# Decay attention followed by a feed-forward layer: q and k loads issued earlier, second product two units behind the first and by halves of the tokens

## The chip, the cores and the metric

The kernel runs on one core of a Trainium2 chip. The metric is device microseconds of one execution. The profile is of one profiled execution of the same program. Names of engines in the profile: PE (TensorE matmul), PEld (its weight loads), DVE (VectorE), ACT (ScalarE), POOL (GpSimd), SP (SyncE, which issues all the DMAs here).

## The reference

Eight batches of eight heads, 576 tokens, head size 64. The attention output, 4608 tokens of 512, goes through a feed-forward layer with 2048 hidden units.

```python
# q, k, v: (8, 8, 576, 64); f: (8, 8, 576)
scores = np.matmul(q, k.transpose(0, 1, 3, 2)) / np.sqrt(64)
cum = np.cumsum(np.log(np.clip(f, 1e-4, 1.0)), axis=-1)
scores = np.where(causal, -1e9, scores + cum[..., :, None] - cum[..., None, :])
attn = np.exp(scores - scores.max(-1, keepdims=True))
x = (attn / (attn.sum(-1, keepdims=True) + 1e-9)) @ v   # -> (4608, 512)
h = x @ w_in                                            # (4608, 2048)
g = np.where(h >= 1, h, np.where(h <= -1, 0, (h + 1) ** 2 / 4))
out = g @ w_out                                         # (4608, 512)
```

## The kernel before, in words

**Attention by jobs.** A job is one pair of heads of one batch (in batch 0 the rows are cut in two, so that there are 36 jobs: eight in batch 0, four in each later batch). The first jobs compute in float32. From job 12 on, q and k are quantized into a high and a low half in float16. For such a job the steps are:

- `load` (L326) brings q and k into one of two float32 buffers, `qk32[ji % 2]`, with six DMAs: for q two of L347 and one of L351, for k the same.
- `measure` (L390) sums the squares of q and of k on ACT (L397, one instruction each, which writes `m2q`); PE adds them over the partitions (L128), and DVE makes a scale of it (L129 to L137). Its result is `sc`.
- `prepare` (L408) quantizes: ACT writes the high halves (L414, two instructions on q and k with the scale `sc`), DVE the low halves (L416), and one DMA transpose brings both into `qkT` (L421). After L416 the q and k buffer is free for the load after the next.
- `load_decay` (L355) brings one head's row of the sums of the log decay to all partitions as `ck` (three buffers); `split_values` (L427) loads v (two DMAs of L440, one of L442) and splits it (L447 on ACT, L448 on DVE).
- For each of five row blocks `r`, `scores` (L459) multiplies q and k into PSUM (tile `s`, two buffers) and has POOL write decay and causal mask (L488, L492) into `sdr` (four buffers) or `sd4` (two, for the last block). `weights` (L557) adds both and takes the row minimum on DVE (L571, which writes `nm`), exponentiates on ACT (L575), makes the reciprocal of the sum on DVE (L583, L586, `rc`), and writes the weights' high half on ACT (L589) and low half on DVE (L595) into `pr`. A DMA transpose (L601, for the last block two of L604) turns them into `pT`, of which there is one buffer.
- `values` (L608) multiplies with v (L615) and writes the result into `x` (L624, L625).

**Feed-forward by units.** A unit is 256 tokens (a chunk) by 256 hidden units (a block), eight units to a chunk, 144 in all. `moe_front` (L642) is the first product, 24 matmuls of 256 columns (48 shorter ones where a chunk lies in two batches) into PSUM tile `ph` (L657). Then comes the chain ACT L666 (relu), ACT L667 (square), DVE L668 (which is the last to read `ph`), ACT L670 (high half of `g`), DVE L671 (low half of `g`). `moe_back` (L678) is the second product: twelve matmuls of 512 columns (L685) from `g` into two PSUM tiles `po0` and `po1`, one for each half of the chunk's tokens, summed over the chunk's eight units. After the last, ACT evicts both (L702) and the chunk is stored (L705). `ph` has two buffers, shared with the sums over partitions (L118, L128); `g` has two; `po0` and `po1` one each.

**What sets the order.** `moe_unit` (L710) issues the first product of a unit and then the second product of the unit before. The loop over jobs (L759) issues, in job `p`: the load of job `p + 2`, `prepare` of job `p + 1`, the row blocks of job `p`, after the last of them `measure` of job `p + 2`, and between the row blocks `values` of job `p - 1` and a share of the units whose tokens are ready: four a job in most batches, six in some. What is left of the units follows after the last job. This is the order in which the code is written. A list scheduler in the framework then sets the order on each engine: it takes the instructions in the order of the code, but lets one whose inputs and buffers are free (by its own estimate) go ahead of one that has to wait. On the chip each engine then follows its list, and SP issues the DMAs in the order of its own.

Of the kernel before, what the change touches and what calls it, by code (L numbers as in the profile page):

```python
# [8 lines left out]
F32 = mybir.dt.float32  # L9
F16 = mybir.dt.float16  # L10
I32 = mybir.dt.int32
AF = mybir.ActivationFunctionType
ALU = mybir.AluOpType
AX = mybir.AxisListType

P = 128
# [29 lines left out]
def kernel(  # L46
# [19 lines left out]
    nc = tc.nc  # L66
# [80 lines left out]
    def decay_sums():  # L147
        fl = early
        nb = B * H
        nc.sync.dma_start(fl[0:nb, 0:S], f.rearrange("b h s -> (b h) s"))  # L150
        nc.vector.tensor_scalar(
            out=fl[0:nb, 0:S], in0=fl[0:nb, 0:S], scalar1=1e-4, scalar2=1.0, op0=ALU.max, op1=ALU.min
        )
        nc.scalar.activation(fl[0:nb, S:2 * S], fl[0:nb, 0:S], AF.Ln)
        nc.gpsimd.memset(fl[0:nb, 3 * S:4 * S], 0.0)
        cum = fl[0:nb, 2 * S:3 * S]
        nc.vector.tensor_tensor_scan(
            out=cum, data0=fl[0:nb, S:2 * S], data1=fl[0:nb, 3 * S:4 * S], initial=0.0, op0=ALU.add, op1=ALU.add
        )
        nc.sync.dma_start(cum_d, cum)  # L160
        pt = ps.tile([P, 1024], F32, name="s")
        twice = fl[0:nb, 0:P]
        nc.vector.tensor_copy(
            twice.rearrange("p (a b) -> p a b", a=2), cum[:, FULL:S].unsqueeze(1).broadcast_to([nb, 2, 64])
        )
        for t in range(NT5):
            nc.tensor.transpose(
                pt[:, nb * t:nb * t + nb], cum[:, P * t:P * t + P] if t < LAST else twice, ident[0:nb, 0:nb]
            )
        nc.vector.tensor_copy(cq.rearrange("p t n -> p (t n)"), pt[:, 0:NT5 * nb])  # L170

# [197 lines left out]
    squares = bits.bitcast(F16)[:, 0:2 * NT5 * D]  # L369
    cq8 = const.tile([P, NT5, 2 * H], F32, name="cq8")  # L370

    def early_prepare(w):

        if w.p == 0:
            nc.vector.tensor_scalar(out=cq8, in0=cq[:, :, 0:2 * H], scalar1=8.0, scalar2=None, op0=ALU.mult)
        t_ = early_qk[(w.p + NQK) % 2]
        w.nsig, w.nalpha = -8.0, -0.125
        bh = w.b * H + 2 * w.hp
        w.cqs = cq8[:, :, bh:bh + 2]
        w.terms = ((t_[:, 0], t_[:, 1]),)  # L380
# [9 lines left out]
    def measure(w):  # L390
# [14 lines left out]
        w.cqs = tiny.tile([P, NT5, 2], F32, name="cqs")  # L405
        nc.vector.tensor_scalar(out=w.cqs, in0=cq[:, :, bh:bh + 2], scalar1=w.nsig, scalar2=-1.0, op0=ALU.mult, op1=ALU.mult)

# [234 lines left out]
    def moe_front(ch, fb):  # L642
# [25 lines left out]
        nc.vector.scalar_tensor_tensor(out=u, in0=h, scalar=z.t[:, i:i + 1], in1=u, op0=ALU.max, op1=ALU.min)  # L668
        g = two.tile([P, 2, 2 * TC], F16, name="g")
        nc.scalar.activation(g[:, 0], u, AF.Copy, scale=z.r[:, i:i + 1])  # L670
# [7 lines left out]
    def moe_back(ch, fb, g, z):  # L678
        first, last, part = z.first == fb, z.last == fb, z.first > 0
        if first:  # L680
            po[ch] = [ps1.tile([P, DM], F32, name=f"po{i}") for i in range(2)]
        for fi in range(2):
            for i in range(2):
                for gl, wl in ((0, 0), (0, 1), (1, 0)):
# [25 lines left out]
    def moe_unit(ch, fb):  # L710
        pending.append(moe_front(ch, fb))
        if len(pending) > 1:
            moe_back(*pending.pop(0))
# [43 lines left out]
    value_scale(0)  # L757
    split_values(pairs[0])
    for p in range(njobs + 1):  # L759
        w = pairs[p] if p < njobs else None  # L760
        nxt = pairs[p + 1] if p + 1 < njobs else None
        steps = []
        if w:
            if w.b not in xs:
                xs[w.b] = xpool.tile([P, NPAIR, 2, S], F16, name="x")
            if p + 2 < njobs:
                pairs.append(load(p + 2))
            if nxt:
# [4 lines left out]
            def step(r):  # L773
                if r + 1 < w.r1:
                    scores(w, r + 1)
                if r == w.r1 - 2 and nxt:
                    load_decay(nxt, 1)
                    split_values(nxt)
                weights(w, r)
                if w.r1 == NT5 and w.b + 1 < B:  # L780
                    n = w.r1 - w.r0
# [69 lines left out]
```

## Time and profile before

| | |
|---|---|
| median of 3 runs | 1209.1 us (1208.8 to 1213.09) |
| profiled execution | 1206.77 us, span 1205.0 us |
| PE busy | 1047.8 us (87%) |
| ACT busy | 795.6 us (66%) |
| DVE busy | 789.7 us (66%) |
| POOL busy | 418.1 us (35%) |
| granted clock of TensorE, mean | 0.94 |
| DMA, hardware queue | 150.63 MB, 57.7% of 16 engines' span |

How to read it: PE's share is a mean over unlike stretches. Up to about 210 us the weights are converted and the first jobs run, and PE is busy for 132.48 us of 210. From there to about 1050 us jobs and units run side by side. The rest is units alone. A row of the waits gives engine, tile and line of the one that waited, the one that it waited for, the total in us, how often, and the longest. In a timeline row stand start and duration in us, then engine, line, operation, tiles, shape, count, and in brackets the idle time ahead of it with the one that ended it.

### The profile page before, as it was taken

The page shows a single profiled execution, that of the slowest core. Times are in us where ns is not written, and L with a number is a line of the kernel's source. Part 1 is how long each engine was busy: PE and PEld are TensorE (multiplying, and loading weights), DVE is VectorE, ACT ScalarE, POOL GpSimd, SP SyncE. Part 2 cuts the span into 40 slices and gives each one's busy share as a digit, 9 for nine tenths or more (in the row PEclk, how much of TensorE's full clock was granted, in tenths as well). Part 3 has the DMA queues.
Part 4 walks back from the last instruction along what each step waited for, and adds up shares of the span by engine and source line. Part 5 has one row for each costly group of instructions (what it writes and reads, how often), then busy time and mean ns, then how long its engine had stood idle before and what let it go on. Part 6 is the DMA issues. An engine that isn't in the chain of part 4 may idle for free. (4 is left out here: it accounts for less than half of the span.)

```text
span 1205.0 us, 24383 instructions
## 1 busy us (share of the span) xinstructions
PE 1047.8 (87%) x8809; PEld 664.8 (55%) x8809; DVE 789.7 (66%) x2103; ACT 795.6 (66%) x1638; POOL 418.1 (35%) x679
## 2 busy tenths in 40 slices
PE   4666765988978889898898998999898999999998
PEld 2433443554645556555655655555565566667665
DVE  5769989787767667765566666676677686532222
ACT  4566876577867677776566667777677686644443
POOL 4467764234533233333213323342343343100000
PEclk9666888998989999998999999999899999999999
DMA  7868788479857566854633745675668575300000
GB/s 226 271 173 243 166 208 180 111 160 181 170 118 169 113 134 127 155 112 111 126 69 76 144 87 130 117 155 116 129 127 149 106 139 105 73 19 1 18 18 18
DMA packets 408281, 152.18 MB, mean 126 GB/s; under 512 B 383968, under 2 KB 384992, under 8 KB 408160
## 3 DMA queue, kind: packets, MB, share of 16 engines
q1 hardware_dynamic: 408160, 150.63, 57.7%
q8 instruction: 69, 1.13, 0.4%
q14 instruction: 52, 0.43, 0.1%
HBM read 75.64 MB, written 9.58 MB: 71 GB/s over the span
## 5 line engine op out<-in xcount | busy, mean ns | idle before, releaser
L685 PE MATMUL po<-place,g 128*128 128x512 f16 x1728 | 429.5, 393 | 55.0 <-ACT g L670 39.4
L657 PE MATMUL ph<-x,place 128*128 128x256 f16 (+3 forms) x4608 | 420.7, 248 | 24.0 <-DVE u L668 24.0
L657 PEld LDWEIGHTS <-place 128*128 128x128 f16 x4608 | 354.2, 98 | 94.2 <-issue 38.5
L685 PEld LDWEIGHTS <-g 128*128 128x128 f16 x1728 | 165.0, 100 | 245.2 <-ACT g L670 56.3
L488 POOL TENSOR_SCALAR sdr<-ck,nsig,cqs 128x128 f32<-128x128 f32 (+1 forms) x192 | 147.3, 771 | 151.2 <-DVE pr L595 148.7
L575 ACT ACTIVATE sdr<-sdr,nm 128x384 f32<-128x384 f32 (+1 forms) x248 | 137.9, 557 | 75.9 <-DVE nm L571 75.3
L668 DVE SCALAR_TENSOR_TENSOR u<-ph,z,u 128x512 f32<-128x512 f32 x136 | 101.6, 747 | 129.4 <-ACT u L667 129.2
L488 POOL TENSOR_SCALAR sd<-ck,nsig,cqs 64x576 f32<-64x576 f32 x48 | 44.2, 921 | 341.6 <-ACT sdr L575 191.6
L666 ACT ACTIVATE u<-ph,z 128x512 f32<-128x512 f32 x136 | 104.4, 768 | 88.0 <-PE ph L657 88.0
L482 PE MATMUL s<-qkT 64*64 64x512 f16 (+11 forms) x1056 | 129.6, 351 | 35.3 <-DVE nm L571 24.9
L595 DVE SCALAR_TENSOR_TENSOR pr<-sdr,rc,pr 128x384 f16<-128x384 f32 (+2 forms) x232 | 129.9, 596 | 41.1 <-ACT pr L589 40.1
L670 ACT ACTIVATE g<-u,z 128x512 f16<-128x512 f32 x136 | 97.8, 719 | 79.0 <-DVE u L668 76.1
L671 DVE SCALAR_TENSOR_TENSOR g<-u,z,g 128x512 f16<-128x512 f32 x136 | 108.0, 794 | 56.6 <-ACT g L670 56.2
L589 ACT ACTIVATE pr<-sdr,rc 128x384 f16<-128x384 f32 (+1 forms) x236 | 118.5, 554 | 10.9 <-issue 6.5
L571 DVE CUSTOM_DVE_ANT_0 sdr<-s,sdr,nalpha 128x128 f32<-128x128 f32 (+1 forms) x192 | 99.4, 545 | 15.9 <-POOL sdr L492 14.6
L492 POOL TENSOR_SCALAR_AFFINE_SELECT sdr<-sdr 128x128 f32<-128x128 f32 x248 | 91.0, 379 | 9.0
L667 ACT ACTIVATE u<-u 128x512 f32<-128x512 f32 x144 | 89.9, 624 | 2.6
L397 ACT ACTIVATE bits<-qk 128x640 f16<-128x640 f32 x48 | 35.0, 729 | 76.1 <-DMA qk<-in_q_dram 75.5
L615 PE MATMUL s<-pT,vs 128*64 128x320 f16 (+3 forms) x1098 | 76.2, 287 | 4.9 <-DMA pT<-pr 4.3
L583 DVE TENSOR_SCALAR rc<-sm 128x2 f32<-128x2 f32 (+1 forms) x149 | 25.9, 174 | 74.4 <-ACT sdr L575 68.4
L615 PEld LDWEIGHTS <-vs 128*64 128x64 f16 x1098 | 50.1, 113 | 33.2 <-issue 15.9
L488 POOL TENSOR_SCALAR sdr<-ck,cq 128x384 f32<-128x384 f32 (+3 forms) x56 | 45.0, 804 | 61.5 <-DVE pr L595 30.2
(155 smaller groups left out, 989.8 us busy)
## 6 DMA issues: line engine op xcount, KB each, us to landing
ck<-cum_d SPq DMA_DIRECT2D x64, 288.0 KB, 3.9
out_dram<-ot SPq DMA_DIRECT2D x36, 256.0 KB, 2.1
qk<-in_k_dram SPq DMA_DIRECT2D x64, 128.0 KB, 3.2
vst<-in_v_dram SPq DMA_DIRECT2D x28, 288.0 KB, 3.2
v<-in_v_dram SPq DMA_DIRECT2D x62, 128.0 KB, 2.7
qk<-in_q_dram SPq DMA_DIRECT2D x56, 128.0 KB, 2.8
place<-in_moe_w_in_dram SPq DMA_DIRECT2D x6, 1024.0 KB, 7.0
place<-in_moe_w_out_dram SPq DMA_DIRECT2D x5, 1024.0 KB, 8.1
```

The costliest lines, as they stand in the source:

```text
L482: nc.tensor.matmul(sds[h % len(sds)][1][p0:p1, c0:c1], lhsT=a[rows, q0 - w.s0:q0 - w.s0 + p1 - p0], rhs=b[rows, c0:c1], start=(i == 0), st ...
L488: nc.gpsimd.tensor_scalar(out=sd[p0:p1, 0:wid], in0=w.ck[h][p0:p1, 0:wid], scalar1=w.nsig if w.p < NQK else w.nsig[p0:p1], scalar2=w.cqs[p ...
L571: nc.vector.tensor_tensor_reduce(out=a, in0=sp[:, 0:wid], in1=a, scale=w.nalpha, scalar=BIG, op0=ALU.add, op1=ALU.min, accum_out=nm[:, i:i ...
L575: nc.scalar.activation(a, a, AF.Exp, bias=nm[:, i:i + 1], scale=-1.0, accum_out=sm[:, i:i + 1])
L589: nc.scalar.activation(pr[:, :, 0, i, :], a, AF.Copy, scale=rc[:, i:i + 1])
L595: nc.vector.scalar_tensor_tensor(out=pr[:, :, 1, i, :], in0=a, scalar=rc[:, i:i + 1], in1=pr[:, :, 0, i, :], op0=ALU.mult, op1=ALU.subtract,)
L615: nc.tensor.matmul(av[64 * h:64 * h + 64, at + s0:at + s1], lhsT=w.vs[:, vl, h, t, :], rhs=w.pT[:, t, pl, h, s0:s1], start=(t == 0 and pi ...
L657: nc.tensor.matmul(ph[:, fi, a0:a1], lhsT=wi[fb][:, wl, t, fi * P:(fi + 1) * P], rhs=xs[b][:, t, xl, s0:s0 + a1 - a0], start=(fi == 0 and ...
L666: nc.scalar.activation(u, h, AF.Relu, scale=z.u[:, i:i + 1], bias=z.h[:, i:i + 1])
L668: nc.vector.scalar_tensor_tensor(out=u, in0=h, scalar=z.t[:, i:i + 1], in1=u, op0=ALU.max, op1=ALU.min)
L671: nc.vector.scalar_tensor_tensor(out=g[:, 1], in0=u, scalar=z.r[:, i:i + 1], in1=g[:, 0], op0=ALU.mult, op1=ALU.subtract)
L685: nc.tensor.matmul(po[ch][i], lhsT=g[:, gl, fi * TC + i * P:fi * TC + (i + 1) * P], rhs=wo[fb][:, wl, fi, :], start=(first and fi == 0 and ...
```

## The change

Five edits.

1. `moe_unit` keeps two units pending instead of one, so a second product is issued after the first products of the two following units; `g` gets a third buffer.
2. In `moe_back` the loop over the two halves of the chunk's tokens is outside, that over the two halves of the block inside: `po0` gets its six matmuls first, then `po1`.
3. The load of job `p + 3` is written after the first row block of job `p`; before, the load of job `p + 2` stood at the start of job `p`. The buffers are the same two, by the job's number. The third load is written ahead of the loop.
4. The sums of the decay are scaled by 8 where they are copied (L170), and the copy `cq8` for batch 0 goes; L406 scales by -0.125 where it did by -1.
5. Lines shift by one or two: the changed kernel's L396 is L397 here, L413 is L414, L420 is L421, L656 is L657, L684 is L685, and so on; of the loads, L349 is L347 and L353 is L351.

```diff
-        nc.vector.tensor_copy(cq.rearrange("p t n -> p (t n)"), pt[:, 0:NT5 * nb])
+        nc.vector.tensor_scalar(
+            out=cq.rearrange("p t n -> p (t n)"), in0=pt[:, 0:NT5 * nb], scalar1=8.0, scalar2=None, op0=ALU.mult
+        )
...
-        if w.p == 0:
-            nc.vector.tensor_scalar(out=cq8, in0=cq[:, :, 0:2 * H], scalar1=8.0, scalar2=None, op0=ALU.mult)
...
-        w.cqs = cq8[:, :, bh:bh + 2]
+        w.cqs = cq[:, :, bh:bh + 2]
...
-        g = two.tile([P, 2, 2 * TC], F16, name="g")
+        g = two.tile([P, 2, 2 * TC], F16, name="g", bufs=3)
...
-        for fi in range(2):
-            for i in range(2):
+        for i in range(2):
+            for fi in range(2):
                 for gl, wl in ((0, 0), (0, 1), (1, 0)):
...
         pending.append(moe_front(ch, fb))
-        if len(pending) > 1:
+        if len(pending) > 2:
             moe_back(*pending.pop(0))
...
+    pairs.append(load(2))
     for p in range(njobs + 1):
...
-            if p + 2 < njobs:
-                pairs.append(load(p + 2))
...
                 weights(w, r)
+                if r == w.r0 and p + 3 < njobs:
+                    pairs.append(load(p + 3))
```

What the scheduler makes of it on the engines is shown at three places.

On PE, in the tail, where a second product begins; the numbers of `ph` go up by 44 from unit to unit, and a `g` has the number of its `ph` plus 29. Before:

```order
L657 MATMUL ph_15144<-x_12323,place_90 128x256
L657 LDWEIGHTS place_90
L657 MATMUL ph_15188<-x_12323,place_90 128x256
L685 LDWEIGHTS g_15129
L685 MATMUL po0_14998<-place_90,g_15129 128x512
L685 LDWEIGHTS g_15129
L685 MATMUL po0_14998<-place_90,g_15129 128x512
L685 LDWEIGHTS g_15129
L685 MATMUL po1_14999<-place_90,g_15129 128x512
```

Now, at the same place:

```order
L656 LDWEIGHTS place_90
L656 MATMUL ph_15130<-x_12315,place_90 128x256
L684 LDWEIGHTS g_15071
L684 MATMUL po0_15028<-place_90,g_15071 128x512
L684 LDWEIGHTS g_15071
L684 MATMUL po0_15028<-place_90,g_15071 128x512
L684 LDWEIGHTS g_15071
L684 MATMUL po0_15028<-place_90,g_15071 128x512
```

Before, the `g` of the unit directly ahead of the finished `ph_15144` is read (15129 = 15100 + 29), and the scheduler mixes matmuls of the next first product in; now that of two units ahead of `ph_15130` (15071 = 15042 + 29), without mixing, and `po0` first.

On SP, between two jobs' DMA transposes of the weights `pT`, in a batch with four units a job (`qk_0_98` is one of the two buffers of q and k). Before:

```order
L604 DMA_TRANSPOSE pT<-pr_9926 128x10x64 x2
L440 DMA v_100<-in_v_dram 128x4x64 x2
L442 DMA v_100<-in_v_dram 64x2x64
L347 DMA qk_0_98<-in_q_dram 128x4x64 x2
L421 DMA_TRANSPOSE qkT<-qs 128x20x128
L358 DMA ck<-cum_d 128x576
L351 DMA qk_0_98<-in_q_dram 64x2x64
L347 DMA qk_0_98<-in_k_dram 128x4x64 x2
L351 DMA qk_0_98<-in_k_dram 64x2x64
L358 DMA ck<-cum_d 128x576
```

Now:

```order
L603 DMA_TRANSPOSE pT<-pr_9918 128x10x64 x2
L439 DMA v_100<-in_v_dram 128x4x64
L349 DMA qk_0_98<-in_q_dram 128x4x64
L420 DMA_TRANSPOSE qkT<-qs 128x20x128
L349 DMA qk_0_98<-in_q_dram 128x4x64
L353 DMA qk_0_98<-in_q_dram 64x2x64
L349 DMA qk_0_98<-in_k_dram 128x4x64 x2
L353 DMA qk_0_98<-in_k_dram 64x2x64
L439 DMA v_100<-in_v_dram 128x4x64
L441 DMA v_100<-in_v_dram 64x2x64
L360 DMA ck<-cum_d 128x576 x2
```

The q and k loads stand around the same transpose of `qkT` as before; one of the three v loads, the rest of v and both `ck` have moved behind them.

On ACT, where one job's quantizing L414 comes up, in the same batch. Before:

```order
L666 ACTIVATE u<-ph,z 128x512
L667 ACTIVATE u<-u 128x512
L670 ACTIVATE g<-u,z 128x512
L575 ACTIVATE sdr_101,sm_10892<-sdr_101,nm 128x128
L575 ACTIVATE sdr_102,sm_10892<-sdr_102,nm 128x128
L575 ACTIVATE sdr_103,sm_10922<-sdr_103,nm 128x256
L575 ACTIVATE sdr_104,sm_10922<-sdr_104,nm 128x256
L414 ACTIVATE qs<-qk_0_98,sc 128x640 x2
```

Now:

```order
L665 ACTIVATE u<-ph,z 128x512
L666 ACTIVATE u<-u 128x512
L669 ACTIVATE g<-u,z 128x512
L413 ACTIVATE qs<-qk_0_98,sc 128x640 x2
L665 ACTIVATE u<-ph,z 128x512
L574 ACTIVATE sdr_101,sm_10878<-sdr_101,nm 128x128
L574 ACTIVATE sdr_102,sm_10878<-sdr_102,nm 128x128
```

The exponentials of the first two row blocks stood between a unit's `g` and the quantizing; now they come behind it, and the next unit's L665 stands between.

More of the change, by code (lines that the diff above doesn't have):

```diff
@@ L369 @@
     squares = bits.bitcast(F16)[:, 0:2 * NT5 * D]
-    cq8 = const.tile([P, NT5, 2 * H], F32, name="cq8")
     def early_prepare(w):
-        if w.p == 0:
-            nc.vector.tensor_scalar(out=cq8, in0=cq[:, :, 0:2 * H], scalar1=8.0, scalar2=None, op0=ALU.mult)
         t_ = early_qk[(w.p + NQK) % 2]
@@ L405, in measure @@
         w.cqs = tiny.tile([P, NT5, 2], F32, name="cqs")
-        nc.vector.tensor_scalar(out=w.cqs, in0=cq[:, :, bh:bh + 2], scalar1=w.nsig, scalar2=-1.0, op0=ALU.mult, op1=ALU.mult)
+        nc.vector.tensor_scalar(out=w.cqs, in0=cq[:, :, bh:bh + 2], scalar1=w.nsig, scalar2=-0.125, op0=ALU.mult, op1=ALU.mult)
     def prepare(w):
```

## The prediction

> **What bounds the kernel now.** I read the stretches of the span first: busy time of each engine, granted clock (PEclk), DMA share.
>
> ```profile
> span 1205.0 us, 24383 instructions
> core 0: us, PE busy (x) PEld busy (x) DVE busy (x) ACT busy (x) POOL busy (x), PEclk, DMA share, GB/s
> 210.00:300.00 90.00, 82.16 (x602) 48.13 (x603) 71.57 (x218) 63.40 (x139) 32.85 (x59) 0.92 0.71 149
> 300.00:544.00 244.00, 216.63 (x2067) 137.92 (x2066) 170.54 (x500) 175.53 (x379) 91.95 (x160) 0.97 0.69 138
> 544.00:714.60 170.60, 156.09 (x1355) 101.01 (x1354) 99.09 (x267) 108.97 (x220) 45.81 (x80) 0.96 0.49 99
> 714.60:960.00 245.40, 219.81 (x1896) 136.15 (x1894) 167.58 (x473) 175.78 (x376) 92.68 (x160) 0.97 0.64 128
> 960.00:1050.00 90.00, 90.00 (x903) 58.23 (x901) 65.58 (x165) 66.18 (x137) 27.65 (x48) 1.00 0.60 115
> 1050.00:1200.00 150.00, 149.52 (x1234) 102.87 (x1233) 42.80 (x57) 63.71 (x91) 0.00 (x0) 1.00 0.03 12
> ```
>
> After 960 PE is never idle and its clock is full: nothing can be won there, and whatever is saved earlier moves the end by as much, since the same units are left for the tail. Between 300 and 960 PE is idle for 27.4 + 14.5 + 25.6 = 67.5 us. The middle stretch (544 to 714.6) holds jobs with six feed-forward units each, the two beside it jobs with four. PE's waits from 300 to 960 say for whom:
>
> ```profile
> PE po L685 <- ACT g L670: 33.2, 15, 6.3
> PE ph L657 <- DVE u L668: 17.4, 12, 3.2
> PE po L685 <- ACT ot L702: 14.7, 4, 4.3
> ```
>
> These are 65.3 of the 67.5 us: the chain from a first product to its `ph` and `g`, and the eviction of a finished chunk. The scores and values hardly wait. So I asked what ACT waits for, in 300 to 544, 544 to 714.6 and 714.6 to 960:
>
> ```profile
> ACT bits L397 <- DMA qk<-in_q_dram: 29.5, 8, 5.4
> ACT g L670 <- DVE u L668: 15.2, 18, 1.5
> ACT u L666 <- PE ph L657: 3.5, 3, 1.4
> ACT vs L447 <- PE s L615: 1.2, 3, 0.5
> ```
> ```profile
> ACT bits L397 <- DMA qk<-in_q_dram: 16.2, 4, 5.0
> ACT u L666 <- PE ph L657: 12.6, 8, 3.5
> ```
> ```profile
> ACT bits L397 <- DMA qk<-in_q_dram: 29.0, 8, 4.5
> ACT g L670 <- DVE u L668: 13.1, 16, 1.0
> ACT u L666 <- PE ph L657: 4.5, 4, 1.4
> ACT vs L447 <- PE s L615: 3.1, 3, 1.4
> ```
>
> Twenty jobs, twenty waits of the measuring L397 for q: 74.7 us, 3.7 each. In the timeline of one job, what this does to PE:
>
> ```profile
> 915.45 0.74 ACT L397 ACTIVATE bits<-qk 128x640 f16<-128x640 f32 x1 [4.49 <-DMA qk<-in_q_dram]
> 920.64 0.75 DVE L668 SCALAR_TENSOR_TENSOR u<-ph,z,u 128x512 f32<-128x512 f32 x1 [0.60 <-ACT u L667]
> 921.44 2.34 PE L657 MATMUL ph<-x,place 128*128 128x256 f16 x20 [3.19 <-DVE u L668]
> ```
>
> ACT stands 4.49 us for q, the work queued behind it (the unit's L666 and L667 among it) is late, and 6 us on PE stands 3.19 us for the `ph` that DVE then frees. The same job as ACT sees it (its window, then its waits):
>
> ```profile
> 902.30:930.40 28.10, 23.84 (x194) 14.56 (x192) 20.01 (x69) 20.90 (x45) 11.58 (x20) 1.00 0.77 142
> ACT bits L397 <- DMA qk<-in_q_dram: 4.5, 1, 4.5
> ACT sdr L575 <- DVE nm L571: 1.9, 3, 0.9
> ACT g L670 <- DVE u L668: 0.8, 1, 0.8
> ```
>
> 20.9 busy + 4.5 + 1.9 + 0.8 = 28.1 us, the whole job, and no wait for PE in it. In a four-unit job ACT's own queue sets the length; PE, with 23.8 us of work, has the idle time left over. In the six-unit stretch ACT waits 12.6 us for L657: there PE sets it. A later job, which has nothing left to load or measure, shows both full:
>
> ```profile
> 965.70:992.90 27.20, 27.20 (x316) 18.07 (x314) 21.87 (x57) 21.75 (x47) 11.74 (x20) 1.00 0.70 137
> ```
>
> **The change part by part.**
>
> *Second product two units behind.* By the rows above and below, a first product takes 2.8 us (20 matmuls in 2.34) and a second 2.7 (4 in 1.04, each next one some 0.85 later).
>
> ```profile
> L666 ACT ACTIVATE u<-ph,z 128x512 f32<-128x512 f32 x136 | 104.4, 768 | 88.0 <-PE ph L657 88.0
> L667 ACT ACTIVATE u<-u 128x512 f32<-128x512 f32 x144 | 89.9, 624 | 2.6
> ```
>
> From the end of a first product `ph` is free after 0.77 + 0.62 + 0.75 = 2.1 us, and `g` begins to be usable some 0.7 later, at 2.9, if ACT is at hand. Today PE has one first product (2.8) before it wants that `g`, which leaves nothing over, and 5.5 before it wants that `ph`, 3.4 over. With two units between, it has 11.0 and 8.2: 8 and 6 us over. A stall of ACT of 3.7 us then no longer reaches PE by itself. This frees PE; it frees ACT only where ACT waits for PE.
>
> *Halves of the tokens.* The same twelve matmuls in another order; the first half of the output is finished six matmuls (about 1.3 us) earlier, so the four chunk evictions (14.7 us) lose some 1.3 us each. At the very end one eviction lies beside matmuls: about 1 us.
>
> *The third `g` buffer, cq8 gone, cq scaled once:* one small DVE operation less and none more, in a start that other work sets. Nothing.
>
> *Loads a job sooner.* They do not move by a job. In both orders SyncE issues a job's q and k right behind the previous reader of that buffer, around the same qkT transpose, and ACT has L397 some dozen instructions behind the same quantizing L414. What moves is who stands ahead of the last q on SP. Its rows in a job:
>
> ```profile
> 934.29 0.62 SPq L442 DMA_DIRECT2D v<-in_v_dram  x1
> 935.66 3.35 SPq L421 DMA_TRANSPOSE qkT<-qs  x1
> 939.88 0.46 SPq L358 DMA_DIRECT2D ck<-cum_d  x1
> 940.39 0.62 SPq L351 DMA_DIRECT2D qk<-in_q_dram  x1
> ```
>
> One of two v issues (like L442, 0.6), L442 and ck (0.46) now come behind q: 1.7 us plus the issue gaps, more where L442 itself is slow. I take 2.0 of the 3.7 us, between 0 (q's landing set by the traffic in the transpose, not by its issue) and all 3.7. What passes behind: ck lands 2 us later (below), v is read by L447 only near a job's end.
>
> *A new wait.* In the new ACT order the L414 of a job follows a `g` copy directly, where exponentials stood between; on DVE the scale that L414 needs comes behind that unit's L671:
>
> ```profile
> 712.38 0.75 DVE L671 SCALAR_TENSOR_TENSOR g<-u,z,g 128x512 f16<-128x512 f32 x1
> 713.05 0.16 DVE L136 TENSOR_SCALAR pw<-pw 128x2 f32<-128x2 f32 x1
> ```
>
> 0.75 + 0.16 + about 0.2 for the reciprocal gives 1.2 us a job that ACT waits, 0 to 2. Against it, L670 stands directly behind its L667 once a job, not two or three times (34 waits, 28.3 us, in the 16 four-unit jobs): about half of these go, 14 us.
>
> *Clock.* By PEclk (0.97, 0.96, 0.97) 7.3 + 6.8 + 7.4 = 21.5 us were withheld between 300 and 960, behind such gaps:
>
> ```profile
> 763.10 1.85 PE L685 MATMUL po<-place,g 128*128 128x512 f16 x4 [2.67 <-ACT g L670]
> 924.31 1.04 PE L685 MATMUL po<-place,g 128*128 128x512 f16 x4 [0.52 <-ACT g L670]
> ```
>
> Four matmuls take 1.85 us instead of 1.04 after a gap of only 2.67 us. The Trainium skill (TensorE: Matmul & The Clock Gate, Part 1) has the clock halve after an idle window of about 3.4 us; by that alone a 2.67 us gap would cost nothing and the withheld time would be smaller. The row decides, and it speaks against reading the page as a threshold on one gap.
>
> **The sum**, against the profiled execution (1206.77 us, its span and 1.8 around it; the median shown is 2.3 us above):
> - Six-unit stretch, PE sets it: 14.5 idle + 6.8 of clock = 21.3 to be had. ACT could give 12.6 + 4 x 2.0 = 20.6. One chunk boundary stays: 16.
> - Four-unit stretches (489.4 us, 16 jobs), ACT sets them: 16 x 2.0 = 32 of q's wait, 14 of L670's, its waits for PE 3.5 + 1.2 + 4.5 + 3.1 = 12, less 16 x 1.2 = 19 of the new wait: 39. PE could give 27.4 + 25.6 + 14.7 = 67.7, so it stays idle for some 28.
> - 210 to 300: 7.8 idle, of which I take 3. The last eviction: 1.
> - Before 210 another order of loads, either way: 0, at most 8.
>
> 16 + 39 + 3 + 1 = 59: 1206.8 - 59 = 1148 us.
>
> **Rivals.**
> *ACT's queue keeps its wait.* If q lands no sooner, the 32 go, and the six-unit stretch gives 12.6 instead of 16: 59 - 32 - 3.4 = 23.6, 1183 us. For it: both halves of the wait hang on the same transpose. Against it: three issues really leave the path. The Trainium skill says it as a rule (TensorE: Matmul & The Clock Gate, Part 1, engine queue depths): ScalarE and VectorE are strict FIFO. The 4.49 us row agrees: work not needing q stood behind it.
>
> *PE becomes the bound everywhere.* If the wait goes whole and ACT's queue has room, all idle time and clock between 300 and 960 go, with 3 at the ends: 67.5 + 21.5 + 3 = 92, 1115 us. For it: the job at 965.7, full on PE at 21.75 us of ACT. Against it: 28.1 us of ACT's queue against 23.8 of PE in the job at 902.
>
> *Slower: ck too late.* Both ck now stand behind k and v; the first is issued some 2 us later than now (two q, three k and two v issues of about 0.6 stand between the transpose and it, 4 us, less the 2 by which the queue ahead of it is shorter). POOL has this in hand behind it:
>
> ```profile
> 919.69 0.68 POOL L488 TENSOR_SCALAR sdr<-ck,nsig,cqs 128x128 f32<-128x128 f32 x1 [3.12 <-DVE pr L595]
> ```
>
> Beyond 3.1 us each further us delays the next job's masks, DVE's L571 and ACT's exponentials, 20 times. The break-even is 59 / 20 + 3.1 = 6.1 us; at 7 us late it would be 20 x 3.9 = 78 lost against 59, 1226 us.
>
> **How the numbers follow.** Forecast 0.50 (1132 to 1165 by its own bounds: 1 us more or less of q's wait in 16 jobs); wait kept 0.22; PE bound 0.18; ck 0.05; the rest, a few per cent, an order that trades one wait for another and ends where it began. The range reaches most of the way to both of the first two rivals: 1118 to 1186. Half a per cent (6 us) is about what a measurement of this kernel can tell from no change: faster 0.88, same 0.06, slower 0.06.
>
> **What would show it.** Right: PE's waits for `g` and `ph` between 300 and 960 rare and under 2 us each; the measuring activation's wait for q near 35 us in total; a new wait of the quantizing activation for DVE's scale, about 20 us; PE idle some 30 us there, PEclk near 1.00. Wrong: q's wait still 75 us (wait kept), or PE without idle time (PE bound), or POOL's wait for ck over 8 us a job with DVE's L571 waiting for POOL (ck).

## The result, and the profile after

The changed kernel takes 1128.61 us (median of 4 runs, 1127.8 to 1130.18), the kernel before 1208.95 in the same comparison (1205.07 to 1213.09). The ratio is 0.9337, with a 95% interval of 0.9304 to 0.9369: faster by 6.6%, some 80 us. Forecast were 1148.0, and 1118 to 1186 as the range. So direction and range were right, and the gain was put at 59 us instead of 80.

In what follows "the jobs" is the part of the span in which jobs with measured scales run beside units. Its stretches are cut where a job's quantizing begins: four-unit, six-unit and four-unit jobs again. Busy time by stretch, first of before with this cut (221, 171 and 251 us), then of after (198, 148 and 224 us):

```profile
323.00:544.00 221.00, 195.60 (x1811) 123.61 (x1809) 152.23 (x444) 156.42 (x335) 80.56 (x140) 0.97 0.67 134
544.00:715.00 171.00, 156.49 (x1356) 101.18 (x1355) 99.40 (x269) 109.37 (x221) 45.94 (x81) 0.96 0.49 99
715.00:966.00 251.00, 225.41 (x1943) 140.18 (x1942) 173.01 (x493) 179.57 (x385) 92.60 (x161) 0.97 0.65 130
```
```profile
span 1126.0 us, 24406 instructions
core 0: us, PE busy (x) PEld busy (x) DVE busy (x) ACT busy (x) POOL busy (x), PEclk, DMA share, GB/s
317.00:515.00 198.00, 190.42 (x1840) 125.43 (x1838) 158.14 (x438) 154.62 (x332) 84.54 (x140) 0.99 0.64 150
515.00:663.00 148.00, 147.04 (x1336) 96.44 (x1334) 101.14 (x271) 107.03 (x219) 46.41 (x80) 1.00 0.49 112
663.00:887.00 224.00, 218.41 (x1973) 141.04 (x1971) 180.25 (x495) 177.04 (x385) 93.83 (x160) 1.00 0.67 147
```

The spans differ by 1205.0 - 1126.0 = 79 us. Ahead of the jobs 323 - 317 = 6 us went, in the jobs 643 - 570 = 73, and behind them nothing (1205 - 966 and 1126 - 887 are both 239). Within the 73, PE's idle time fell from 65.5 to 14.1 us, which is 51. By the PEclk column 21 us of clock were withheld before (0.03 x 221 + 0.04 x 171 + 0.03 x 251) and 2 after, which is 19. So 70 of the 73 us are idle time of PE and the clock that went with it.

What PE still waits for at the units in the jobs, its waits at the scores left out (245 to 912 us of after). The wait for ACT's half of `g`, 33.2 us before, is not in this list any more, and that for the eviction has gone from 14.7 to 0.7 us:

```profile
PE ph L656 <- DVE u L667: 9.7, 13, 1.8
PE po L684 <- ACT ot L701: 0.7, 1, 0.7
PE po L684 <- DVE g L670: 0.5, 2, 0.3
```

The group of the second product's matmuls, of before and of after: fewer idle microseconds in front (last part), and 383 ns for one instead of 393.

```profile
L685 PE MATMUL po<-place,g 128*128 128x512 f16 x1728 | 429.5, 393 | 55.0 <-ACT g L670 39.4
```
```profile
L684 PE MATMUL po<-place,g 128*128 128x512 f16 x1728 | 404.8, 383 | 7.9 <-ACT g L669 6.7
```

ACT's largest waits for DMA and DVE in the two four-unit stretches, before (323 to 544 and 715 to 966 us):

```profile
ACT bits L397 <- DMA qk<-in_q_dram: 27.3, 7, 5.4
ACT g L670 <- DVE u L668: 15.2, 18, 1.5
ACT sdr L575 <- DVE nm L571: 11.0, 19, 1.5
ACT sd L575 <- DVE nm L571: 1.2, 3, 0.5
...
ACT bits L397 <- DMA qk<-in_q_dram: 29.0, 8, 4.5
ACT sdr L575 <- DVE nm L571: 15.1, 24, 1.5
ACT g L670 <- DVE u L668: 14.3, 17, 1.1
ACT sd L575 <- DVE nm L571: 1.9, 2, 1.6
```

and after (317 to 515 and 663 to 887 us):

```profile
ACT bits L396 <- DMA qk<-in_q_dram: 8.5, 6, 1.9
ACT g L669 <- DVE u L667: 8.2, 10, 1.1
ACT bits L396 <- DMA qk<-in_k_dram: 6.7, 6, 2.3
ACT qs L413 <- DVE sc L137: 6.4, 6, 1.1
ACT sdr L574 <- DVE nm L570: 5.6, 7, 1.0
ACT sd L574 <- DVE nm L570: 3.5, 3, 1.2
...
ACT bits L396 <- DMA qk<-in_q_dram: 11.7, 8, 2.2
ACT qs L413 <- DVE sc L137: 9.9, 9, 1.1
ACT g L669 <- DVE u L667: 6.8, 8, 1.0
ACT sdr L574 <- DVE nm L570: 6.1, 6, 1.0
ACT bits L396 <- DMA qk<-in_k_dram: 4.9, 7, 1.6
ACT sd L574 <- DVE nm L570: 4.5, 4, 1.2
```

The measuring activation's wait for q fell from 56.3 to 20.2 us, and a wait for k of 11.6 us has come up behind it. How q came sooner is seen in one job of each: the measuring activation with its wait (before, then after), and for after SyncE's rows around the transpose, with the issue of both `ck`. Of before, the SyncE rows of the same job are in the prediction.

```profile
944.15 0.74 ACT L397 ACTIVATE bits<-qk 128x640 f16<-128x640 f32 x1 [4.02 <-DMA qk<-in_q_dram]
```
```profile
805.69 1.00 SPq L349 DMA_DIRECT2D qk<-in_q_dram  x2
806.79 2.55 SPq L420 DMA_TRANSPOSE qkT<-qs  x1
809.38 0.62 SPq L353 DMA_DIRECT2D qk<-in_q_dram  x1
811.74 0.74 ACT L396 ACTIVATE bits<-qk 128x640 f16<-128x640 f32 x1 [1.18 <-DMA qk<-in_q_dram]
813.22 2.02 SPq L360 DMA_DIRECT2D ck<-cum_d  x2
```

From the start of the transpose to the issue of the last part of q it was 940.39 - 935.66 = 4.73 us, now it is 809.38 - 806.79 = 2.59: `ck` no longer stands between, two parts of q and not one went ahead of the transpose, and the transpose itself held SyncE for 2.55 us here, not 3.35. The shorter transpose does not come from the order of the loads; the last section says what it goes with.

### The profile page after: what moved, and what is told of

Its sections match the earlier page's. It is cut to its first block, busy times and chain, and to the rows that moved or that the text cites. A ratio compares the mean times of both kernels' runs of the same rounds, so it can differ in the third digit from the quotient of the medians.

```text
span 1126.0 us, 24406 instructions
## 1 busy us (share of the span) xinstructions
PE 1020.5 (91%) x8809; PEld 662.4 (59%) x8809; DVE 803.2 (71%) x2102; ACT 787.8 (70%) x1638; POOL 427.5 (38%) x679
## 4 chain that ended last, share of the span: by engine, by line
PE 34%; ACT 15%; DVE 7%; DMA 3%; SPq 3%; issue 2%; ACTq 0%; DVEq 0%
PE po L684 15%; PE ph L656 15%; ACT sdr L574 4%; DMA qk<-in_k_dram 3%; ACT pr L588 2%; SPq L349 2%; ACT g L669 2%; PE s L614 2%; ACT u L666 2%; PE s L481 2%; DVE qs L415 2%; ACT u L665 1%; DVE u L667 1%; DVE pr L594 1%; ACT bits L396 1%
## 5 line engine op out<-in xcount | busy, mean ns | idle before, releaser
L656 PE MATMUL ph<-x,place 128*128 128x256 f16 (+3 forms) x4608 | 417.9, 249 | 19.3 <-DVE u L667 16.5
L684 PE MATMUL po<-place,g 128*128 128x512 f16 x1728 | 404.8, 383 | 7.9 <-ACT g L669 6.7
L656 PEld LDWEIGHTS <-place 128*128 128x128 f16 x4608 | 355.7, 99 | 82.0 <-issue 33.9
L684 PEld LDWEIGHTS <-g 128*128 128x128 f16 x1728 | 167.2, 100 | 184.5 <-ACT g L669 9.2
L487 POOL TENSOR_SCALAR sdr<-ck,nsig,cqs 128x128 f32<-128x128 f32 (+1 forms) x192 | 157.1, 822 | 163.5 <-DVE pr L594 152.4
L665 ACT ACTIVATE u<-ph,z 128x512 f32<-128x512 f32 x136 | 104.3, 767 | 83.9 <-PE ph L656 83.8
L481 PE MATMUL s<-qkT 64*64 64x512 f16 (+11 forms) x1056 | 119.9, 341 | 33.8 <-DVE nm L570 20.8
L594 DVE SCALAR_TENSOR_TENSOR pr<-sdr,rc,pr 128x384 f16<-128x384 f32 (+2 forms) x232 | 132.6, 605 | 21.3 <-ACT pr L588 19.7
L670 DVE SCALAR_TENSOR_TENSOR g<-u,z,g 128x512 f16<-128x512 f32 x136 | 105.0, 772 | 53.4 <-ACT g L669 52.8
L614 PE MATMUL s<-pT,vs 128*64 128x320 f16 (+3 forms) x1098 | 71.5, 282 | 7.2 <-DMA pT<-pr 6.0
L487 POOL TENSOR_SCALAR sdr<-ck,cq 128x384 f32<-128x384 f32 (+3 forms) x56 | 45.5, 813 | 65.5 <-DVE pr L594 28.1
L396 ACT ACTIVATE bits<-qk 128x640 f16<-128x640 f32 x48 | 35.2, 734 | 44.7 <-DMA qk<-in_q_dram 25.5
L481 PEld LDWEIGHTS <-qkT 64*128 64x128 f16 (+1 forms) x864 | 32.8, 99 | 56.6 <-issue 39.0
```

The lines of the kernel that those rows point to most:

```text
L481: nc.tensor.matmul(sds[h % len(sds)][1][p0:p1, c0:c1], lhsT=a[rows, q0 - w.s0:q0 - w.s0 + p1 - p0], rhs=b[rows, c0:c1], start=(i == 0), st ...
L487: nc.gpsimd.tensor_scalar(out=sd[p0:p1, 0:wid], in0=w.ck[h][p0:p1, 0:wid], scalar1=w.nsig if w.p < NQK else w.nsig[p0:p1], scalar2=w.cqs[p ...
L594: nc.vector.scalar_tensor_tensor(out=pr[:, :, 1, i, :], in0=a, scalar=rc[:, i:i + 1], in1=pr[:, :, 0, i, :], op0=ALU.mult, op1=ALU.subtract,)
L614: nc.tensor.matmul(av[64 * h:64 * h + 64, at + s0:at + s1], lhsT=w.vs[:, vl, h, t, :], rhs=w.pT[:, t, pl, h, s0:s1], start=(t == 0 and pi ...
L656: nc.tensor.matmul(ph[:, fi, a0:a1], lhsT=wi[fb][:, wl, t, fi * P:(fi + 1) * P], rhs=xs[b][:, t, xl, s0:s0 + a1 - a0], start=(fi == 0 and ...
L665: nc.scalar.activation(u, h, AF.Relu, scale=z.u[:, i:i + 1], bias=z.h[:, i:i + 1])
```

## The experiments

Before is in each comparison the kernel before on the same chip (medians 1211.95, 1208.65 and 1207.72 us for the three groups of four runs below).

| run | median, us (range) | ratio to before, 95% interval |
|---|---|---|
| `ahead_only` | 1140.78 (1139.2 to 1143.3) | 0.9411, 0.9385 to 0.9437 |
| `loads_only` | 1155.04 (1152.89 to 1157.91) | 0.9521, 0.9490 to 0.9552 |
| `no_halves` | 1129.51 (1128.79 to 1130.71) | 0.9317, 0.9294 to 0.9340 |
| `old_loads` | 1139.69 (1137.88 to 1140.12) | 0.9397, 0.9373 to 0.9421 |
| `late_before` | 1132.08 (1129.98 to 1133.5) | 0.9342, 0.9311 to 0.9373 |
| `late_after` | 1113.8 (1113.36 to 1115.29) | 0.9196, 0.9162 to 0.9231 |
| `more_before` | 1206.31 (1204.74 to 1209.79) | 0.9978, 0.9956 to 1.0000 |
| `more_after` | 1138.45 (1137.81 to 1139.49) | 0.9397, 0.9367 to 0.9426 |
| `early_before` | 1131.75 (1130.39 to 1133.92) | 0.9370, 0.9339 to 0.9400 |
| `tie_only_after` | 1110.61 (1109.14 to 1111.2) | 0.9191, 0.9163 to 0.9219 |
| `late_ahead` | 1113.08 (1111.92 to 1114.46) | 0.9214, 0.9180 to 0.9248 |
| `late_loads` | 1128.42 (1127.59 to 1129.01) | 0.9340, 0.9312 to 0.9368 |

The theory was that of the prediction: ACT stands still at the measuring activation for q, PE loses what is queued behind it, and the change shortens this wait (order of the loads on SyncE) and hides the rest from PE (two units behind). The rivals: PE or another wait sets the pace, or only one of the edits does anything.

### One edit at a time

**`ahead_only`**: the changed kernel with the loads and the halves as before. What is left, beside the scaling of the decay sums:

```diff
-        g = two.tile([P, 2, 2 * TC], F16, name="g")
+        g = two.tile([P, 2, 2 * TC], F16, name="g", bufs=3)
...
-        if len(pending) > 1:
+        if len(pending) > 2:
```

> The second product two units behind and the third g buffer alone; loads where they stood, halves of the block outside. Theory (ACT's queue sets the four-unit jobs, and both edits are needed): the six-unit stretch gets its whole gain (23 us by the changed kernel's job starts), the four-unit jobs only the part that is ACT's waits for PE, so 1150 to 1170 us, with ACT still waiting over 50 us for q. Rival (the two units of cover are all, ACT's wait is a symptom): 1128 to 1135 us. Rival (the loads are all): 1195 to 1209 us.

**`loads_only`**: the changed kernel with one unit pending and the old halves. What is left, beside the scaling of the decay sums and the third `g` buffer:

```diff
+    pairs.append(load(2))
     for p in range(njobs + 1):
...
-            if p + 2 < njobs:
-                pairs.append(load(p + 2))
...
+                if r == w.r0 and p + 3 < njobs:
+                    pairs.append(load(p + 3))
```

> The loads written earlier alone; second product one unit behind, halves of the block outside (the third g buffer stays, unused). Theory: ACT's wait for q falls from 75 us to about 35, PE's idle time after it by as much, and the clock follows: 1150 to 1175 us. Rival (two units of cover are all): 1200 to 1209 us. Rival (the loads are all): 1128 to 1135 us.

**`no_halves`**: the changed kernel with the old order of the second product's matmuls.

```diff
-        for i in range(2):
-            for fi in range(2):
+        for fi in range(2):
+            for i in range(2):
```

> The changed kernel with the halves of the block outside again. Theory: the order within twelve matmuls matters only at chunk boundaries and at the end, 0 to 6 us slower than the changed kernel: 1128 to 1135 us. Rival (the halves carry a third of the gain, since the evictions were 14.7 us and each cost clock behind it): 1145 to 1155 us.

**`old_loads`**: the changed kernel with the loads where they were.

```diff
-    pairs.append(load(2))
     for p in range(njobs + 1):
...
+            if p + 2 < njobs:
+                pairs.append(load(p + 2))
...
-                if r == w.r0 and p + 3 < njobs:
-                    pairs.append(load(p + 3))
```

> The changed kernel with the loads where they stood (two units behind, third g buffer and halves kept). Theory: as the kernel with two units alone, less the evictions: 1145 to 1165 us, ACT waiting over 50 us for q. Rival (two units of cover are all): 1128 to 1133 us, whatever ACT waits for q.

Measured: two units behind give 5.9%, the loads 4.8%, all edits together 6.6%. But both kernels also have the scaling of the decay sums and the third `g` buffer, and no kernel with these alone was run. So what each of the two edits gives by itself, and how far they stand in for each other, is not shown. Taken out of the changed kernel, the loads are worth 0.6% (`old_loads`), the two units together with the halves 1.8% (`loads_only`). The halves give nothing that can be measured: 0.9317 without them, 0.9337 with them. `loads_only` and `no_halves` came out where the theory had them; `ahead_only` and `old_loads` came out better, between the theory and the rival that the two units are all. ACT's and PE's waits of the whole `ahead_only` run show two things that may account for it:

```profile
ACT bits L396 <- DMA qk<-in_q_dram: 42.2, 20, 4.2
```
```profile
PE ph L656 <- DVE u L667: 18.0, 16, 4.1
PE po L684 <- ACT g L669: 7.2, 10, 3.0
```

ACT still stands 2.1 us a job for q, up to 4.2, and PE notices it less: it waits 7.2 us for `g` in the whole span, where before it was 33.2 in the jobs alone, and in the jobs it is idle for 22.5 us of 578 (65.5 of 643 before). That is the cover of two units. But q's wait has also fallen, from 3.7 us to 2.1 a job, though no load was moved in the code: the scheduler made a new order for SyncE, with both `ck` behind k, and the transpose ahead of q is shorter (last section). So no edit of this kernel can be switched off without the others' order changing a little, and the shares above are those of whole orders.

### Taking ACT's wait for q away

**`late_before`**: the kernel before, with the measuring activation given a factor of one which DVE works out from the third row block of the job two ahead of the one that is measured.

```diff
+        w.rcs = {}
...
-    def measure(w):
+    def measure(w, of):
...
+        w.sc = sc = tiny.tile([P, 2], F32, name="sc")
+        tie = sc[:, 0:1]
+        nc.vector.tensor_scalar(out=tie, in0=of, scalar1=0.0, scalar2=1.0, op0=ALU.mult, op1=ALU.add)
...
-            nc.scalar.activation(squares, w.x32[j], AF.Square, accum_out=m2[:, j:j + 1])
-        w.sc = sc = tiny.tile([P, 2], F32, name="sc")
+            nc.scalar.activation(squares, w.x32[j], AF.Square, scale=tie, accum_out=m2[:, j:j + 1])
...
+        w.rcs[r] = rc[:, 0:1]
...
-                    measure(pairs[p + 2])
+                    measure(pairs[p + 2], w.rcs[min(w.r0 + 2, w.r1 - 1)])
```

> The kernel before, with one edit: the measuring activation takes a factor of one that DVE works out from the third row block's reciprocal of the job before, so it comes some ten instructions later in ACT's queue, when q and k have long landed. Second product still one unit behind, loads where they were. Theory (ACT's wait for q, 74.7 us, is what makes PE idle and sets the four-unit jobs): the waits for q and k fall to under 8 us in all, PE's idle time between jobs 4 and 23 falls from 65 us to under 25, and the time to 1140 to 1160. Rival (it is the cover of only one unit between the two products that makes PE idle; the wait for q is one of several stalls that hit it): the waits for q go, others come up in their place (g for DVE, exp for nm), PE stays idle for 40 us or more, and the time is 1170 to 1195.

**`late_after`**: the same edit in the changed kernel.

> The changed kernel with the same one edit as late_before. Its ACT still waits 43 us for q and k, in 36 waits. Theory of the prediction (in a four-unit job ACT's own queue sets the length): with those waits gone the fifteen four-unit jobs lose some 2 us each until PE is full, 14 us, so 1110 to 1117. Rival (with two units between the products PE sets these jobs too, and ACT's waits only fill its slack): 1122 to 1131, with ACT's waits moving to PE's ph or DVE's u.

**`early_before`**: as `late_before`, tied to the second row block.

```diff
-                    measure(pairs[p + 2], w.rcs[min(w.r0 + 2, w.r1 - 1)])
+                    measure(pairs[p + 2], w.rcs[min(w.r0 + 1, w.r1 - 1)])
```

> The kernel before with the edit of late_before, but tied to the second row block instead of the third: the measuring activation now comes five or six instructions sooner in ACT's queue than in the kernel before, and SyncE's order stays as it was. So only the length of ACT's wait for q is raised. Theory (the stall of ACT at the measuring activation goes into the four-unit jobs one for one, and on to PE): the wait rises from 3.7 to about 6.5 us a job, 20 jobs, and the time to 1245 to 1270. Rival (the stall is only one of several, and other waits give way, as the additional work of more_before was absorbed): 1205 to 1225.

**`tie_only_after`**: the changed kernel with the tie of `early_before`, meant as a control.

> Control: the changed kernel with the same tie as late_after, but to the second row block, which leaves the measuring activation and everything else on ACT and SyncE where the changed kernel has it. If the place of the instruction is what gained 15 us in late_after: 1126 to 1132, and ACT's waits for q and k stay at 40 to 50 us. If the tie itself (one small DVE instruction a job) does something: outside that.

Measured: `late_before` 0.9342, `early_before` 0.9370. One added dependency in the kernel before gives as much as the whole change (0.9337), and more than the theory expected of `late_before` (1140 to 1160 us). Both expectations on `early_before`, and that on the control, were wrong, because I had read the place of the measuring activation in ACT's queue by its distance from the quantizing and not by its buffer. ACT's rows in before and in `early_before`, two jobs each:

```text
before         632 L414 ACTIVATE qs<-qk_1_99,sc 128x640 x2
               643 L397 ACTIVATE bits,m2q<-qk_1_99 128x640
               675 L414 ACTIVATE qs<-qk_0_98,sc 128x640 x2
               686 L397 ACTIVATE bits,m2q<-qk_0_98 128x640
early_before   671 L417 ACTIVATE qs<-qk_0_98,sc 128x640 x2
               677 L401 ACTIVATE bits,m2q<-qk_1_99,sc 128x640
               714 L417 ACTIVATE qs<-qk_1_99,sc 128x640 x2
               720 L401 ACTIVATE bits,m2q<-qk_0_98,sc 128x640
```

Before, ACT measures the buffer that it has just quantized from: the load that fills it again has only now been issued. The scheduler had hoisted the measuring by a whole job, as its inputs were free by its estimate. The tie forbids that: the measuring reads the other buffer, which was loaded one job ago. The trace of `early_before` says the same. Here are one job's rows on ACT and, of SyncE, the load of the buffer just quantized:

```profile
862.54 1.53 ACT L417 ACTIVATE qs<-qk,sc 128x640 f16<-128x640 f32 x2
866.02 0.82 ACT L401 ACTIVATE bits<-qk,sc 128x640 f16<-128x640 f32 x1
...
872.05 0.62 SPq L352 DMA_DIRECT2D qk<-in_q_dram  x1
```

The measuring runs without a wait at 866.02, six microseconds before the last part of q is issued. Its stretches, cut by job as above, and PE's waits for `ph` and for ACT's `g` in 244 to 917 us:

```profile
323.00:517.00 194.00, 189.98 (x1832) 124.36 (x1831) 153.34 (x457) 158.40 (x338) 82.29 (x141) 1.00 0.78 151
517.00:669.00 152.00, 150.03 (x1357) 99.58 (x1356) 99.03 (x271) 109.70 (x219) 45.39 (x81) 1.00 0.55 112
669.00:889.00 220.00, 216.75 (x1939) 139.76 (x1938) 172.26 (x499) 180.24 (x383) 94.95 (x160) 0.99 0.74 148
```
```profile
PE ph L661 <- DVE u L672: 7.2, 5, 2.0
...
PE po L689 <- ACT g L674: 1.4, 1, 1.4
```

The second product is one unit behind here, SyncE's order of the loads is that of before, and the transpose is as long (median 3.4 us in both). ACT has as much to do as before (338.6 us in the four-unit stretches, 336.0 before). Yet PE waits 1.4 us for `g` and is idle for 9 us of 566, where it was idle for 65.5 us of 643. So the wait of ACT for q made PE's gaps: with the single unit of distance left as it was, they are gone. The place on ACT to which the measuring goes matters little: two ties, to the second and to the third row block, give nearly the same. The Trainium skill (TensorE: Matmul & The Clock Gate, Part 1, on the engine queue depths) calls ScalarE strictly first in, first out; these runs agree with it, since one waiting instruction a job, with what stands behind it, cost 77 us (1208.65 - 1132.08 in `late_before`).

In the changed kernel the tie gives 0.9196 and 0.9191: the best versions, about 15 to 18 us below the change. Here are the stretches of `tie_only_after`:

```profile
317.00:505.00 188.00, 186.36 (x1819) 121.96 (x1818) 159.93 (x452) 155.65 (x332) 86.31 (x140) 1.00 0.72 156
505.00:653.00 148.00, 148.00 (x1350) 97.48 (x1350) 101.20 (x266) 107.77 (x218) 45.74 (x80) 1.00 0.51 114
653.00:869.00 216.00, 216.00 (x1955) 138.71 (x1954) 180.91 (x507) 178.19 (x385) 102.03 (x160) 1.00 0.68 153
```

PE is idle for 1.6 us of 552, at full clock: the jobs are now bound by PE. A kernel with only the added DVE instruction, and the measuring left in its old job, was not run, so that the instruction by itself gains nothing is argued, not shown; it adds work and no freedom.

### Two units and loads, once the wait is gone

**`late_ahead`** and **`late_loads`**: `ahead_only` and `loads_only` with the edit of `late_before`.

> ahead_only with the edit of late_before: second product two units behind, loads and halves as before the change, and no wait for q. If two units of cover only hide ACT's stall, they add nothing once it is gone: 1128 to 1136, as late_before. If they are worth something by themselves: 1110 to 1120, as late_after.

> loads_only with the edit of late_before: loads written earlier, second product one unit behind, and no wait for q. If the loads' place matters only by ACT's wait for q, it adds nothing once that is gone: 1128 to 1136, as late_before. If it is what separates late_before from late_after: 1110 to 1120.

| ratio to before | as it was | measuring a job later |
|---|---|---|
| the kernel before | 1 | 0.9342 |
| loads | 0.9521 | 0.9340 |
| two units | 0.9411 | 0.9214 |
| all | 0.9337 | 0.9196 |

All rows but the first have the scaling of the decay sums and the third `g` buffer besides. With the wait gone, these and the place of the loads together are worth nothing (0.9340 against 0.9342): the 4.8% of `loads_only` came by way of the wait alone. Two units behind are worth 1.3% even then; the intervals of `late_ahead` lie apart from those of `late_before` and `late_loads`. So the second product's distance was not only a cover for ACT's stall. What these some 15 us are is only in part idle time of PE: between `early_before` and `tie_only_after` (rows above) the jobs go from 566 to 552 us, of which 7.6 are PE's idle time and 6.4 its busy time, 2 of these by the clock, and 6 us more went ahead of the jobs (323 to 317). Why PE is busy for less was not tried.

### More work for ACT

**`more_before`** and **`more_after`**: in each kernel the squares are formed once more, and nobody reads them.

```diff
             nc.scalar.activation(squares, w.x32[j], AF.Square, accum_out=m2[:, j:j + 1])
+        for j in range(2):
+            nc.scalar.activation(squares, w.x32[j], AF.Square)
```

> The kernel before, with two more ACT instructions in each job from 12 on: the sums of squares of q and k are formed once more, 2 x 0.74 us, and nobody reads the result. Theory (ACT's queue sets the four-unit jobs before the change): +1.5 us in each of fifteen four-unit jobs and about half of that in the four six-unit jobs, so 1228 to 1242. Rival (ACT has room behind its waits): under 1220.

> The changed kernel with the same two more ACT instructions in each job as more_before. If ACT's queue still sets the four-unit jobs, as the prediction has it: +1.5 us in fifteen jobs, 1147 to 1155. If PE sets them: 1128 to 1138, and ACT's waits (88 us in the four-unit jobs) become shorter by what the instructions take, about 22 us.

Measured: before, ACT was busy for 795.6 us and is now for 824.2; the time is the same (0.9978). The wait for q, 75.5 us in the whole span of before, is shorter by some of it:

```profile
ACT bits L397 <- DMA qk<-in_q_dram: 63.6, 20, 6.3
```

So the theory failed here: the amount of ACT's work does not set the four-unit jobs, for 28.6 us more of it found room in its waits. In the changed kernel it cost 1138.45 - 1128.61 = 9.8 us, just above the end of what was expected if PE sets the jobs. In both runs the scheduler also made a new order, so the sizes are rough.

## Why the prediction was right, and where it was not

*PE is the measure, and the tail is fixed.* Right: 239 us behind the jobs in both.

*PE idles behind ACT's wait for q.* Right, and shown by `late_before` and `early_before`: without that wait PE's gaps are gone, with one unit of distance and nearly the same work on every engine.

*"In a four-unit job ACT's own queue sets the length."* Not as it was put. The sum 20.9 + 4.5 + 1.9 + 0.8 = 28.1 proves nothing: on an engine that is followed from one instruction to the same one a job later, busy time and waits always add up to the job. `more_before` shows that the work in the sum had room; `early_before` shows that the 4.5 in it was what counted. The term of 39 us for the four-unit stretches was worked out by this rule, so it is in part luck that the time came out within the range.

*Two units behind give cover.* Right: in `ahead_only` PE waits for `g` for 7.2 us while ACT still stands 42.2 us for q. It was read as cover for this one stall; `late_ahead` shows 1.3% besides. The count for the kernel before was wrong. Between the two products of a unit stand the second product of the unit ahead and the next first product, 2.7 + 2.8 = 5.5 us and not 2.8, so `g` had some 2.6 us to spare and not nothing. In the trace of before PE works for 5.9 us at the least between the two (units 27 to 110, median 6.8). In after the median is 11.0, as forecast. A stall of 3.7 us is more than the 2.6 too, so the conclusion did not hang on it. For `ph` the distance did not grow: PE works for 6.0 us at the least between a first product and the one that takes its buffer next, 10.1 in the median, and in after for 6.3 and 9.3.

*Clock.* Right: some 2 us are withheld now where it was 21. A gap's length alone does not tell whether it costs clock: in the prediction's rows four matmuls take 1.85 us after a gap of 2.67, while after the longer gap of 3.19 at 921.44 twenty take 2.34 and the row of that job (902.30 to 930.40) shows a PEclk of 1.00.

*Halves.* Forecast were some 1.3 us for each of a few evictions and 1 us at the end. The tail shows nothing, and `no_halves` is not slower.

*The loads don't move by a job; SyncE's order takes 2.0 us off q's wait.* Right in mechanism: 56.3 / 15 = 3.75 us a job became 20.2 / 15 = 1.35. Of the 2.14 us that went between transpose and last part of q in the job shown, 0.80 are the shorter transpose, which the sum did not have, so that 2.4 us came where 2.0 were forecast is in part luck. And k then came too late in its turn, 11.6 us in all, which the sum did not have: a wait for two transfers in a row was counted only at the first.

*The third `g` buffer and the scaling: nothing.* Open. With the measuring moved, they and the place of the loads together are worth nothing (0.9340 against 0.9342). With the measuring in its old place they may be worth something, since the transposes are shorter in every kernel that has them (last section).

*The new wait for the scale.* Right: 6.4 + 9.9 = 16.3 us in the four-unit stretches, 1.1 at the most; 19 were forecast. *ACT's wait for DVE between square and `g` halves.* Right: 29.5 to 15.0, 14 were forecast.

*The sum.* This is where the 20 us were lost:

| part, us | forecast | measured |
|---|---|---|
| ahead of the jobs | 3 | 6 |
| six-unit stretch | 16 | 171 - 148 = 23 |
| four-unit stretches | 39 | 472 - 422 = 50 |
| end | 1 | 0 |
| sum | 59 | 79 |

In the six-unit stretch I left one chunk boundary and some idle time standing; in fact all of it went (PE idle for 1.0 us, clock 1.00). Two units are not needed for that: in `early_before`, with one, PE is idle there for 2.0 us. And ACT's wait for PE, of which 12.6 us were counted as to be had, is still there (515 to 663 us of after):

```profile
ACT u L665 <- PE ph L656: 12.5, 8, 2.7
```

In the four-unit stretches the terms came out as: q and k 24.5 of 32; `g` 14.5 of 14; the new wait 16.3 of 19; ACT's waits for PE some 8 of 12. These make 31 where 39 were forecast. What I did not have in the sum made up for it: the exponentials' wait for the row minimum fell by 9.5 (29.2 to 19.7), ACT's own busy time by 4.3 (336.0 to 331.7), and some 5 went in waits smaller than the rows shown. By the point made above this says where ACT's time went, and not what set the length of the jobs. Since the exponentials now stand behind the quantizing instead of ahead of it, DVE has had longer to make their minimum; this is argued from the order and was not tried apart.

*The rivals.* The wait kept: no. The slower one, `ck` too late for POOL: no, its waits for `ck` in the jobs fell, before (245 to 993 us) and after (245 to 912 us):

```profile
POOL sd L488 <- DMA ck<-cum_d: 105.1, 23, 6.0
```
```profile
POOL sd L487 <- DMA ck<-cum_d: 69.8, 22, 5.2
```

In the job shown the first `ck` is issued 813.22 - 806.79 = 6.4 us after the start of the transpose, before it was 939.88 - 935.66 = 4.2: the 2 us of the prediction, which its 3.1 us of slack could take. How much more POOL could have taken was not tried. PE the bound everywhere, 1115 us: this is nearest to what came in the six-unit stretch, and `tie_only_after` (1110.6 us) is that rival come true once ACT's wait is really gone. The change stops 14 us of PE's idle time short of it.

## What to carry to other kernels

When an in-order engine waits for a transfer, look first at which buffer the waiting instruction reads and how soon its result is needed: here it could simply be done a job later, and one dependency gave what five edits did. Distance between producer and consumer hides such a stall; it does not end it, and the two add up only in part. That an engine's busy time and waits add up to a stage's length is true of every engine and says nothing on what bounds the stage; double its work, or take its wait away, to see. And edits that stay in every kernel of an experiment, as the scaling and the third `g` buffer did here, need a kernel of their own.

## What the runs showed that was not expected

With a scheduler that chooses the order by its own estimate of the time, each edit moved instructions on engines that it did not touch: in `ahead_only`, whose code moves no load, `ck` has another place on SyncE. The estimate had let the measuring go ahead by a whole job, into a wait of 3.7 us.

The same bytes can keep the DMA engines busy for very different times. Here is the hardware queue (packets, MB, share of 16 engines' span) in `early_before` with its span of 1128.6 us, and in the changed kernel with 1126.0:

```profile
q1 hardware_dynamic: 408160, 150.63, 62.3%
```
```profile
q1 hardware_dynamic: 408160, 150.63, 56.4%
```

That is 703 against 635 us for equal packets. Worked out in this way, the kernels fall into two groups: 695 to 707 us for the kernel before, `more_before`, `early_before` and `late_before`; 635 to 647 us for the changed kernel and the nine others, wherever their loads and their second product stand. In the same groups a transpose of `qkT` holds SyncE for 3.4 to 3.5 us and for 2.6 to 2.7 us (medians of 24). The order on SyncE is not the reason: in five jobs of `late_ahead` the order around the transpose is that of before, with `ck` between the parts of q, and the transpose takes 2.6 to 2.9 us there, where in before it took 3.25 or more in this order. What all ten have in common, and the other four not, is the scaling of the decay sums without the copy `cq8`, and the third `g` buffer. Which of them does it, and how, was not tried. The DMA engines' time by itself did not show in the kernel's time: 1131.75 us for `early_before`, in the first group, and 1128.42 for `late_loads`, in the second.
